# Layer norm, attention and a gated MLP: another order of the QKV calls, and the norm statistics of two blocks on ScalarE

## The chip, the cores and the metric

The kernel runs on one core of one Trainium2 chip. The metric is device microseconds (us) of one execution. Engine names in the profile: PE is TensorE, PEld its weight loads, DVE is VectorE, ACT is ScalarE, POOL is GpSimd, SP is SyncE (here it only issues DMAs).

## The reference

A layer of 2048 tokens with 576 channels: layer norm, attention of 32 heads in which each token looks at 8 keys (itself and every second token before it), a projection, a residual, then layer norm and a gated MLP of 4608 hidden units with a second residual. All in 32-bit floats.

```python
def _A_ref(x, wqkv, wo):
    H = 32; Dh = D // H            # 18 channels a head
    W, dil = 8, 2
    q, k, v = (x @ wqkv) ...       # split by head
    off = jnp.arange(W) * dil
    idx = pos[:, None] - off[None, :]
    ...
    attn = softmax(where(mask, einsum("bhsd,bhswd->bhsw", q, kg) * scale, -1e9))
    o = jnp.einsum("bhsw,bhswd->bhsd", attn, vg)
    return o... @ wo

def _B_ref(x, w_gate, w_up, w_down):
    return (sigmoid(x @ w_gate) * (x @ w_up)) @ w_down

h = x + _A_ref(_layernorm(x), A_wqkv, A_wo)
h2 = h + _B_ref(_layernorm(h), B_w_gate, B_w_up, B_w_down)
```

## The kernel before, in words

The tokens are split into even and odd ones (a key lies two tokens back, so the two sets never meet) and each set in halves: four blocks of 512 tokens, numbered 0 to 3, blocks 2 and 3 being the odd tokens. A block is four tiles of 128 tokens. Heads go in four groups of eight.

Matrix products are made of 32-bit operands split into a high and a low part (`split`: ACT copies the rounded high part, DVE subtracts it from the source), with three matmuls for each product (`tok_major`).

The stretch before the MLP works like this:

- `ln1(b, xb)` norms block b tile by tile. `ln_j` takes mean and variance on DVE (`bn_stats`, `bn_aggr`) and the power -1/2 on POOL. For blocks 0 and 1 DVE applies them. For blocks 2 and 3 (`on_act`) ACT applies them in two passes, one that subtracts the mean and one that multiplies, and a third short one copies the last 64 columns. Then PE transposes the tile (`tr_main`, `tr_rest`) and ACT and DVE split the result into `th` and `tl`.
- `qkv(b, g, T, w)` is one call: queries, keys and values of head group g for block b, four passes of 14 matmuls with 432 columns. ACT copies each pass to `ev`, and three DMAs of ACT's queue store the call in DRAM. (1, 0) is block 1, head group 0.
- `att_all` is attention as a generator. It takes items in a fixed order: (0,0), (0,1), (1,0), (0,2), (0,3), (1,1), (1,2), (1,3), each after its call. An item fetches its queries, keys (`kw`) and values (`vw`) from DRAM through SP's queue and runs nearly wholly on DVE, with operations of up to 2.6 us. Items of block 1 are spilled to DRAM by a DMA of POOL's queue (`o<-kw`). Between the passes of each call, `step(ag, n)` emits some steps of attention.
- `norm_under(b, xb, call, n)` emits the norm of block b between the passes of a call of another block. `heads` emits calls without a norm beside them.
- The weights of head group 2 can be split only once the last call that uses those of group 0 is emitted, since two groups fit; the same for group 3 after group 1.
- After the second pass of (2,3), `front` projects block 0 (`proj_j`), norms it and stores it (`x<-tok`). Then the MLP starts. Its first weights are loaded early (`wf`), the next (`wg`) by a DMA of POOL's queue. Attention items (1,1) to (1,3) that are not finished run on under the MLP, and block 1 is projected there.

The scheduler orders instructions on each engine by the order of emission, by priority (`tc.high_priority(n)` moves an instruction ahead by n places) and by its own estimate of when operands are ready. On the chip each engine and each DMA queue then runs in that fixed order.

Of the kernel before, what the change touches and what calls it, by code (L numbers as in the profile page):

```python
# [15 lines left out]
F32 = mybir.dt.float32  # L16
F32R = mybir.dt.float32r
AF = mybir.ActivationFunctionType
ALU = mybir.AluOpType
AX = mybir.AxisListType  # L20

P = 128
S = 2048
D = 576
# [6 lines left out]
NS = 4  # L31
TB = P * NS
DM = 512
DR = D - DM
DX = D + DR
# [5 lines left out]
EPS = 1e-5  # L41
# [11 lines left out]
HI = 400  # L53
# [7 lines left out]
def kernel(ctx, tc, x, wqkv, wo, wmlp, out):  # L61
    nc = tc.nc
    dve, act, pool, pe, sp = nc.vector, nc.scalar, nc.gpsimd, nc.tensor, nc.sync
# [9 lines left out]
    sm = ctx.enter_context(tc.tile_pool(name="sm", bufs=2))  # L73
# [12 lines left out]
    mhalf = cst.tile([P, 1], F32, name="mhalf")  # L86
# [16 lines left out]
    def split(hi, lo, src):  # L103
        act.activation(hi, src, AF.Copy)  # L104
        splits.append(dve.tensor_tensor(lo, src, f32(hi), ALU.subtract))  # L105

    def split_rest(t, src):
        act.activation(t, src, AF.Copy)
        dve.tensor_tensor(t[64:128], src[64:128], f32(t[64:128]), ALU.subtract)  # L109

    def pads(g):
        for e in range(2):
            for s in (kscr, vscr):
                a = s[e][g][0:LP, :]
                sp.dma_start(bass.AP(tensor=a.tensor, offset=a.offset,
                                     ap=[[LP * CG // 16, 16], [1, LP * CG // 16]]), zero)

    def ln_j(xj, xn, on_act):
        bs = sm.tile([P, 2, 6], F32, bufs=4, name="bs")
        mv = sm.tile([P, 2], F32, bufs=4, name="mv")  # L120
        rstd = sm.tile([P, 1], F32, bufs=4, name="rstd")
        for k in range(2):
            dve.bn_stats(bs[:, k], xj[:, k * DH2:(k + 1) * DH2])
        dve.bn_aggr(mv, bs)
        dve.tensor_scalar(rstd, mv[:, 1:2], EPS, None, ALU.add)
        pool.tensor_tensor(rstd, rstd, mhalf, ALU.pow)
        if on_act:
            nm = sm.tile([P, 1], F32, bufs=4, name="nm")
            dve.tensor_scalar(nm, mv[:, 0:1], -1.0, None, ALU.mult)
            act.activation(xn[:, :D], xj, AF.Identity, bias=nm)  # L130
            act.activation(xn[:, :D], xn[:, :D], AF.Copy, scale=rstd)
            act.activation(xn[:, D:DX], xn[:, DM:D], AF.Copy)
        else:
            dve.tensor_scalar(xn[:, :D], xj, mv[:, 0:1], rstd, ALU.subtract, ALU.mult)
            dve.tensor_copy(xn[:, D:DX], xn[:, DM:D])

    def tr_main(ps, xn):
        for c in range(4):
            pe.transpose(ps[:, c * P:(c + 1) * P], xn[:, c * P:(c + 1) * P], ident)
        return ps.rearrange("p (c n) -> p c n", c=4)  # L140

    def tr_rest(ps, xn):
        pe.transpose(ps[:, :P], xn[:, DM:DX], ident)
        return ps[:, :P]

    def tok_major(ps, n, th, tl, js, wh, wl):
        k = 0
        for c in range(4):
            for a, m in ((th, wh), (tl, wh), (th, wl)):
                pe.matmul(ps[:, :n], a[:, c, js], m[:, c], start=k == 0, stop=False)  # L150
                k += 1
        pe.matmul(ps[:, :n], th[:, 4, js], wh[:, 4], start=False, stop=False)  # L152
        return pe.matmul(ps[:, :n], th[:, 4, js], wl[:, 4], start=False, stop=True)  # L153
# [71 lines left out]
    def step(gen, n):  # L225
        for _ in range(n):
            if next(gen, END) is END:
                return

    def drain(gen):  # L230
        for _ in gen:
            pass
# [7 lines left out]
    def proj_j(bank, t, wos, th, tl, xn_tile, put, order=(0, 1)):  # L240
        oj = t[0]
        pv = tr_main(bank(), oj)
        with tc.high_priority(HI):
            split(th[:, 0:4], tl, pv)
        yield
        pv = tr_rest(bank(), oj)
        with tc.high_priority(HI):
            split_rest(th[:, 4], pv)
        yield
        for i in order:  # L250
            ps = bank()
            tok_major(ps, DH2, th, tl, slice(0, P), *wos[i])
            hs = t[1][:, i * DH2:(i + 1) * DH2]
            with tc.high_priority(HI):
                dve.tensor_tensor(hs, hs, ps[:, :DH2], ALU.add)
            yield
        xn = xn_tile()
        with tc.high_priority(HI):
            ln_j(t[1], xn, False)
        yield  # L260
        pv = tr_main(bank(), xn)
        with tc.high_priority(HI):
            put(pv, slice(0, 4))
        yield
        pv = tr_rest(bank(), xn)
        with tc.high_priority(HI):
            put(pv.unsqueeze(1), slice(4, 5))
        yield
# [18 lines left out]
    def th_tile():  # L287
        return xt.tile([P, 5, TB], F32R, tag="th", bufs=3, name="th")

    def tl_tile():  # L290
        return xt.tile([P, 4, TB], F32R, tag="tl", bufs=4, name="tl")
# [24 lines left out]
    def mm_tile():  # L316
        return psp.tile([P, 512], F32, tag="mm", bufs=3, name="mm")

    def acc_tile():
        return psp.tile([P, 512], F32, tag="acc", bufs=5, name="acc")  # L320

    def tok_tile(shape=(P, NS, DX)):
        return stk.tile(list(shape), F32, tag="tok", bufs=2, name="tok")

    def th3_tile(dt):
        return sar.tile([P, 5, TB], dt, tag="th3", name="th3")

    def ev_tile(shape):
        return sar.tile(shape, F32, tag="ev", bufs=2, name="ev")

    def load_x(b):
        e, hf = BLOCKS[b]
        t = sah.tile([P, NS, D], F32, bufs=2, name="h")
        for j in range(NS):
            sp.dma_start(t[:, j], xv[e, hf][:, j])
        return t

    def ln1(b, xb):
        th = th3_tile(F32R) if b == 3 else th_tile()
        tl = tl_tile()  # L340
        yield th, tl
        xn = tok_tile()
        for j in range(NS):
            js = slice(j * P, (j + 1) * P)
            pri = 2 * HI if b == 0 else HI if b > 1 else 0
            with tc.high_priority(pri):
                ln_j(xb[:, j], xn[:, j], b > 1)
            pv = tr_main(mm_tile(), xn[:, j])
            pr = tr_rest(acc_tile(), xn[:, j])
            with tc.high_priority(pri):  # L350
                split(th[:, 0:4, js], tl[:, :, js], pv)
                split_rest(th[:, 4, js], pr)
            yield

    def raw_w(g):
        if g == 3:
            wr = sah.tile([P, NS, D], F32, bufs=2, name="h").rearrange("p j d -> p (j d)")
            wr = wr[:, :QC].rearrange("p (c n) -> p c n", c=5)
        else:
            wr = swo.tile([P, 5, NQ], F32, tag="wo", name="wr")  # L360
        for c in range(5):
            sp.dma_start(wr[:, c], wqkv[g][:, c * NQ:(c + 1) * NQ])
        return wr
# [13 lines left out]
    def qkv(b, g, T, w):  # L377
        e, hf = BLOCKS[b]
        ev = ev_tile([P, 3, NS, CG])
        for j in range(NS):  # L380
            ps = acc_tile()
            passes.append(tok_major(ps, NQ, *T, slice(j * P, (j + 1) * P), w[:, 0], w[:, 1]))
            with tc.high_priority(HI):
                act.activation(ev[:, :, j], ps[:, :NQ].rearrange("p (t c) -> p t c", t=3), AF.Copy)  # L384
            yield
        r0 = LP + hf * TB
        with tc.high_priority(HI):
            act.dma_start(qscr[b][g], ev[:, 0].rearrange("p j c -> p (j c)"))
            for t, s in ((1, kscr), (2, vscr)):
                act.dma_start(s[e][g][r0:r0 + TB, :].rearrange("(p j) c -> p (j c)", p=P),  # L390
                              ev[:, t].rearrange("p j c -> p (j c)"))
        emitted.add((b, g))
# [29 lines left out]
    T = []  # L422

    def norm_under(b, xb, call, n):
        gl = ln1(b, xb)
        T.append(next(gl))
        for _ in call:
            step(ag, n)
            next(gl, END)
            step(ag, n)  # L430
        drain(gl)

    def heads(order, ws, n):
        for b, g in order:
            for _ in qkv(b, g, T[b], ws[g]):
                step(ag, n)

    xb = load_x(0)
    w = [qkv_w(0, raw_w(0))]
# [4 lines left out]
    xb = load_x(1)  # L444
# [3 lines left out]
    xb = load_x(2)  # L448
    norm_under(2, xb, qkv(1, 0, T[1], w[0]), 1)
    xb = load_x(3)  # L450
    wr = raw_w(2)
    norm_under(3, xb, qkv(2, 0, T[2], w[0]), 1)
    heads(((3, 0),), w, 2)
    w.append(qkv_w(2, wr))
    wr = raw_w(3)
    pads(2)
    heads(((1, 1), (0, 2), (2, 1), (3, 1)), w, 2)
    w.append(qkv_w(3, wr))
    pads(3)
    h = load_x(0)  # L460
# [649 lines left out]
    for c, (kind, p, f) in enumerate(items):  # L1110
        w, d = wc
# [116 lines left out]
```

## Time and profile before

| | |
|---|---|
| median of three runs | 1589.88 us (1587.89 to 1590.72) |
| profiled execution, first to last instruction (span) | 1589.2 us |
| granted TensorE clock, mean over the span | 0.993 |
| TensorE busy | 1553.3 us |
| VectorE busy | 1268.1 us |
| ScalarE busy | 869.2 us |
| GpSimd busy | 184.2 us |

The profile gives no time for the profiled execution beside its span; the median of the runs lies 0.7 us above that span. The busy time of an engine is a sum over the whole span. A wait names the engine and line that came last. A row of a timeline begins with its start and length in us, and ends with the idle time before it and what ended that, in brackets. "L104" is line 104 of the kernel; lines 104 and 105 are the two halves of `split`, so one line stands for many tiles and the tile's name tells them apart.

### The profile page before, as it was taken

How to read it: one execution, taken by the hardware profiler on the slowest of the kernel's cores; microseconds unless marked ns; L12 is line 12 of the kernel's file. 1: busy time of each engine (PE TensorE's matmuls, PEld its weight loads, DVE VectorE, ACT ScalarE, POOL GpSimd, SP SyncE). 2: the span in 40 equal slices, each digit the busy share in tenths (PEclk: the TensorE clock that was granted, in tenths of full speed). 3: DMA queues.
4: the chain of work that ended last, by engine and by line, in shares of the span. 5: the costliest groups of instructions: out<-in, count | busy, mean ns of one | idle time of the engine just before them, and what ended most of it. 6: DMA issues, size and time to landing. Idle time of an engine off the chain costs nothing.

```text
span 1589.2 us, 22383 instructions
## 1 busy us (share of the span) xinstructions
PE 1553.3 (98%) x8532; PEld 1381.6 (87%) x8532; DVE 1268.1 (80%) x1931; ACT 869.2 (55%) x1546; POOL 184.2 (12%) x230
## 2 busy tenths in 40 slices
PE   7999979999999999999989999999999999999998
PEld 6999968888888888888879988888888888888887
DVE  7999988959999999999546687876677776677755
ACT  4432234425555666656443255776677776677761
POOL 1000000011010001000101100122112112212210
PEclk9999999999999999999999999999999999999999
DMA  7664544346367565665764234899989999989983
GB/s 267 208 206 163 193 184 165 133 177 246 104 164 205 157 170 139 166 191 149 210 203 143 100 110 110 182 186 181 176 169 183 184 173 180 177 170 182 184 170 124
DMA packets 76892, 273.50 MB, mean 172 GB/s; under 512 B 8336, under 2 KB 14224, under 8 KB 75888
## 3 DMA queue, kind: packets, MB, share of 16 engines
q0 software_dynamic: 27792, 105.89, 36.3%
q1 hardware_dynamic: 41360, 146.06, 27.4%
q10 hardware_dynamic: 7632, 20.12, 3.3%
q8 instruction: 67, 1.10, 0.3%
q14 instruction: 41, 0.34, 0.1%
HBM read 145.88 MB, written 128.52 MB: 173 GB/s over the span
## 4 chain that ended last, share of the span: by engine, by line
PE 55%; issue 27%; POOL 7%; DVE 6%; DMA 4%; ACT 1%; SPq 0%; POOLq 0%; ACTq 0%; DVEq 0%
PE b L609 23%; PE dp L723 15%; POOL h L794 7%; PE acc L150 6%; PE b L616 4%; PE b L150 1%; PE bgp L150 1%; DMA wg<-in_wmlp_dram 1%; DVE pr L182 1%; DMA x<-tok 1%; DVE pr L208 1%; DVE lg L186 1%; PE acc L152 1%; DMA tail<-h 1%; PE acc L153 1%
## 5 line engine op out<-in xcount | busy, mean ns | idle before, releaser
L609 PE MATMUL b<-tl,w 128*128 128x512 f32 x1716 | 438.1, 395 | 9.1 <-ACT w L104 6.5
L609 PEld LDWEIGHTS b<-tl,w 128*128 128x128 f32 x1716 | 311.7, 189 | 66.5 <-ACT w L104 7.7
L609 PE MATMUL b<-th,w 128*128 128x512 f32 x1368 | 352.8, 393 | 0.4 <-DVE s L698 0.3
L609 PEld LDWEIGHTS b<-th,w 128*128 128x128 f32 x1368 | 249.8, 188 | 46.7 <-DVE s L698 0.7
L104 ACT ACTIVATE w<-wg 128x640 fp32r<-128x640 f32 (+2 forms) x197 | 117.0, 598 | 125.2 <-PE b L616 59.8
L791 ACT ACTIVATE ev<-dp 128x576 f32<-128x576 f32 x224 | 145.0, 647 | 61.8 <-PE dp L785 58.2
L616 PE MATMUL b<-th,w 128*128 128x512 f32 x572 | 177.0, 391 | 0.0
L794 POOL DMA_DIRECT2D h<-ev x128 | 110.2, 862 | 456.8 <-ACT ev L791 440.5
L105 DVE TENSOR_TENSOR w<-wg,w 128x640 fp32r<-128x640 f32 (+2 forms) x197 | 126.8, 649 | 38.7 <-ACT w L104 38.3
L150 PE MATMUL acc<-qw,th 128*128 128x432 f32 x512 | 155.7, 365 | 1.2 <-DVE th L109 0.9
L105 DVE TENSOR_TENSOR w<-tw,w 128x512 fp32r<-128x512 f32 x116 | 79.6, 687 | 81.1 <-ACT w L104 80.2
L616 PEld LDWEIGHTS b<-th,w 128*128 128x128 f32 x572 | 107.7, 188 | 23.1
L723 PE MATMUL dp<-d,h0h 128*128 128x288 f32 x640 | 119.0, 296 | 1.7 <-DVE tail L733 1.7
L723 PE MATMUL dp<-d,h1h 128*128 128x288 f32 x640 | 120.0, 297 | 0.0
L723 PEld LDWEIGHTS dp<-d,h0h 128*128 128x128 f32 x640 | 99.4, 189 | 5.5 <-DVE tail L733 2.0
L150 PEld LDWEIGHTS acc<-qw,th 128*128 128x128 f32 x512 | 97.2, 190 | 6.5 <-DVE th L109 1.1
L723 PEld LDWEIGHTS dp<-d,h1h 128*128 128x128 f32 x640 | 99.5, 190 | 2.9
L731 ACT ACTIVATE stage<-dp 128x576 f32<-128x576 f32 x96 | 61.7, 646 | 62.4 <-PE dp L723 62.3
L104 ACT ACTIVATE w<-tw 128x512 fp32r<-128x512 f32 x116 | 72.8, 628 | 41.3 <-PE b L609 40.9
L150 PE MATMUL acc<-qw,tl 128*128 128x432 f32 x256 | 92.8, 362 | 0.0
L384 ACT ACTIVATE ev<-acc 128x432 f32<-128x432 f32 x64 | 33.9, 531 | 104.4 <-PE acc L153 97.7
L182 DVE TENSOR_TENSOR pr<-kw,q 128x2304 f32<-128x2304 f32 x32 | 81.7, 2552 | 2.8 <-DMA kw<-k 2.6
(278 smaller groups left out, 2899.8 us busy)
## 6 DMA issues: line engine op xcount, KB each, us to landing
h<-ev POOLq DMA_DIRECT2D x96, 576.0 KB, 7.2
wg<-in_wmlp_dram SPq DMA_DIRECT2D x49, 928.0 KB, 5.2
h<-stage POOLq DMA_DIRECT2D x24, 1152.0 KB, 10.6
wg<-in_wmlp_dram SPq DMA_DIRECT2D x36, 640.0 KB, 4.1
kw<-k SPq DMA_DIRECT2D x16, 792.0 KB, 4.4
vw<-v SPq DMA_DIRECT2D x16, 792.0 KB, 5.5
wd<-in_wmlp_dram SPq DMA_DIRECT2D x18, 576.0 KB, 7.2
h<-ev POOLq DMA_DIRECT2D x32, 288.0 KB, 6.8
```

Of the source, the lines that this page charges most:

```text
L104: act.activation(hi, src, AF.Copy)
L105: splits.append(dve.tensor_tensor(lo, src, f32(hi), ALU.subtract))
L150: pe.matmul(ps[:, :n], a[:, c, js], m[:, c], start=k == 0, stop=False)
L152: pe.matmul(ps[:, :n], th[:, 4, js], wh[:, 4], start=False, stop=False)
L182: dve.tensor_tensor(pr, both(kw, u), q[:, us].unsqueeze(2).broadcast_to([P, 2, W, CG]), ALU.mult)
L384: act.activation(ev[:, :, j], ps[:, :NQ].rearrange("p (t c) -> p t c", t=3), AF.Copy)
L609: pe.matmul(ps, wt[:, a, k0 + c], xx[:, m + c], start=first and k == 0, stop=k == 5, skip_group_check=True)
L616: pe.matmul(ps, wt[:, a, k0], xx[:, 4], start=False, stop=a == 1, skip_group_check=True)
L723: pe.matmul(ps[:, i, :DH2], a[:, js], d[:, m, i * DH2:(i + 1) * DH2], start=k == 0, stop=k == n)
L731: act.activation(hv, ps, AF.Copy)
L791: act.activation(hs[:, k % 2], ps[:, :, :DH2], AF.Copy)
L794: pool.dma_start(hsev[:, u, k0:k + 1], hs[:, :k + 1 - k0], accum_op=ALU.add, max_dma_last_dim=8 * D)
```

## The change

Two things change.

The order of calls: (1,1) is called directly after (1,0), and the norm of block 3 is emitted under it instead of under (2,0). Then follow (2,0) and (3,0), the weights of group 2, and (2,1), (0,2), (3,1). The call (0,2) thereby moves from seventh to eighth place. The other calls keep their place, and attention its order of items.

The norm of blocks 2 and 3: DVE has no part in the statistics any more. ACT makes two passes over the tile that also sum along the row: a copy scaled by -1/576, whose sum is the negative mean, and a square with that mean added, whose sum is 576 times the variance. Their written output is discarded. POOL takes the power and multiplies the mean by it. A third pass of ACT applies both at once. The statistics of a tile are emitted one tile ahead of its scaling. The splits of blocks 2 and 3, and their norm, lose the priority that they had (`HI`).

```diff
-    def ln_j(xj, xn, on_act):
+    def ln_j(xj, xn):
...
-        if on_act:
-            nm = sm.tile([P, 1], F32, bufs=4, name="nm")
-            dve.tensor_scalar(nm, mv[:, 0:1], -1.0, None, ALU.mult)
-            act.activation(xn[:, :D], xj, AF.Identity, bias=nm)
-            act.activation(xn[:, :D], xn[:, :D], AF.Copy, scale=rstd)
-            act.activation(xn[:, D:DX], xn[:, DM:D], AF.Copy)
-        else:
-            dve.tensor_scalar(xn[:, :D], xj, mv[:, 0:1], rstd, ALU.subtract, ALU.mult)
-            dve.tensor_copy(xn[:, D:DX], xn[:, DM:D])
+        dve.tensor_scalar(xn[:, :D], xj, mv[:, 0:1], rstd, ALU.subtract, ALU.mult)
+        dve.tensor_copy(xn[:, D:DX], xn[:, DM:D])
+
+    def ln_stats(xj, junk):
+        mv = sm.tile([P, 2], F32, bufs=4, name="mv")
+        rstd = sm.tile([P, 1], F32, bufs=4, name="rstd")
+        act.activation(junk[:, :D], xj, AF.Copy, scale=-1.0 / D, accum_out=mv[:, 0:1])
+        act.activation(junk[:, :D], xj, AF.Square, bias=mv[:, 0:1], accum_out=mv[:, 1:2])
+        pool.tensor_scalar(rstd, mv[:, 1:2], 1.0 / D, EPS, ALU.mult, ALU.add)
+        pool.tensor_tensor(rstd, rstd, mhalf, ALU.pow)
+        pool.tensor_tensor(mv[:, 0:1], mv[:, 0:1], rstd, ALU.mult)
+        return mv[:, 0:1], rstd
+
+    def ln_scale(xj, nr, xn):
+        act.activation(xn[:, :D], xj, AF.Identity, bias=nr[0], scale=nr[1])
+        act.activation(xn[:, D:DX], xn[:, DM:D], AF.Copy)
...
+        pri = 2 * HI if b == 0 else 0
+        nr = []
         for j in range(NS):
             js = slice(j * P, (j + 1) * P)
-            pri = 2 * HI if b == 0 else HI if b > 1 else 0
+            while b > 1 and len(nr) < min(j + 2, NS):
+                nr.append(ln_stats(xb[:, len(nr)], xn[:, len(nr)]))
             with tc.high_priority(pri):
-                ln_j(xb[:, j], xn[:, j], b > 1)
+                if b > 1:
+                    ln_scale(xb[:, j], nr[j], xn[:, j])
+                else:
+                    ln_j(xb[:, j], xn[:, j])
...
     xb = load_x(3)
+    norm_under(3, xb, qkv(1, 1, T[1], w[1]), 1)
     wr = raw_w(2)
-    norm_under(3, xb, qkv(2, 0, T[2], w[0]), 1)
-    heads(((3, 0),), w, 2)
+    heads(((2, 0), (3, 0)), w, 2)
     w.append(qkv_w(2, wr))
     wr = raw_w(3)
     pads(2)
-    heads(((1, 1), (0, 2), (2, 1), (3, 1)), w, 2)
+    heads(((2, 1), (0, 2), (3, 1)), w, 2)
     w.append(qkv_w(3, wr))
```

More of the change, by code (lines that the diff above doesn't have):

```diff
@@ L258, in proj_j @@
         with tc.high_priority(HI):
-            ln_j(t[1], xn, False)
+            ln_j(t[1], xn)
         yield
```

## The prediction, made before the changed kernel was run

> **What bounds the kernel now.** I read the page first, then the waits of TensorE over the whole span, then windows of the stretch before the MLP, and last the chain and the timelines around the largest wait. From the page:
>
> ```profile
> span 1589.2 us, 22383 instructions
> ...
> PE 1553.3 (98%) x8532; PEld 1381.6 (87%) x8532; DVE 1268.1 (80%) x1931; ACT 869.2 (55%) x1546; POOL 184.2 (12%) x230
> ...
> kw<-k SPq DMA_DIRECT2D x16, 792.0 KB, 4.4
> ```
>
> TensorE (PE) is busy 1553.3 of 1589.2 us. The change neither adds nor removes a matmul, so it can act only on the other 35.9 us and on the granted clock. The waits of PE say where that idle time lies:
>
> ```profile
> PE mm L139 <- DVE tok L134: 9.5, 2, 9.1
> PE b L609 <- ACT w L104: 6.5, 1, 6.5
> ...
> PE b L609 <- DVE s L629: 2.5, 1, 2.5
> PE b L139 <- DMA oj<-o: 2.4, 1, 2.4
> ...
> PE mm L150 <- DVE tl L105: 1.3, 1, 1.3
> PE acc L150 <- DVE th L109: 0.9, 1, 0.9
> ```
>
> The first row is mostly the 9.1 us in which block 0 is loaded and normed; the change does not touch it. In reach are 6.5, 2.5, 2.4, 1.3 and 0.9 us. Windows place them and show the clock (columns: PE, PEld, DVE, ACT and POOL busy, PEclk, DMA share, GB/s):
>
> ```profile
> 20.00:60.00 40.00, 38.88 (x218) 36.37 (x217) 34.95 (x91) 25.23 (x58) 6.47 (x12) 1.00 0.81 278
> ...
> 77.00:181.50 104.50, 104.50 (x535) 99.86 (x534) 99.94 (x87) 29.67 (x63) 0.91 (x1) 1.00 0.54 185
> ...
> 228.00:232.00 4.00, 1.51 (x7) 0.93 (x5) 0.74 (x1) 0.00 (x0) 0.00 (x0) 1.00 0.99 411
> 232.00:236.00 4.00, 0.00 (x0) 0.00 (x0) 2.92 (x2) 3.32 (x5) 0.00 (x0) 0.54 0.89 355
> 236.00:246.00 10.00, 7.46 (x17) 5.57 (x18) 8.66 (x12) 3.10 (x6) 0.00 (x0) 0.50 0.17 44
> ...
> 320.00:326.00 6.00, 6.00 (x33) 5.43 (x32) 2.74 (x4) 1.95 (x4) 0.00 (x0) 0.72 1.01 399
> ```
>
> From 77 to 181.5 us PE is never idle, and VectorE (DVE) is 96% busy beside it. The hole is the hand-over to the MLP: PE stops at 229.5, waits 6.5 us, then 2.5 us more, and the clock is at half until 246. Its 7.46 us of work between 236 and 246 would have taken half that, so the hole costs 6.5 + 2.5 + 3.7 = 12.7 us. The 2.4 us wait before block 1's output projection is followed by 6 us at clock 0.72, or 1.7 us more: 4.1 in all. The chain and timelines show what ends the hole:
>
> ```profile
> 221.19 11.15 DMA x<-tok
> 232.36 0.69 ACT d L104
> ```
>
> ```profile
> 233.06 1.28 ACT L653 ACT_TABLE_LOAD   x1
> ...
> 235.24 2.08 ACT L104 ACTIVATE w<-wg 128x640 fp32r<-128x640 f32 x4 [0.29 <-DMA wg<-in_wmlp_dram]
> ```
>
> ```profile
> 224.00 0.76 POOL L221 DMA_DIRECT2D o<-kw  x1 [12.57 <-DVE kw L219]
> 224.78 0.57 POOL L565 DMA_DIRECT2D wg<-in_wmlp_dram  x1
> ```
>
> ```profile
> DMA packets 1198, 5.43 MB, mean 272 GB/s; under 512 B 144, under 2 KB 144, under 8 KB 1069
> ...
> x<-tok ACTq DMA_DIRECT2D x1, 1280.0 KB, 11.1
> ...
> vw<-v SPq DMA_DIRECT2D x1, 792.0 KB, 5.9
> ...
> o<-kw POOLq DMA_DIRECT2D x1, 288.0 KB, 8.5
> ```
>
> Two transfers gate it, almost together. The store of block 0's normed rows (x<-tok) frees memory that `d` needs, and ScalarE (ACT) stands in order behind that until 232.36. The next MLP weights land at 235.24; POOL issued them only at 224.78, behind the spill of attention (1,1), which waited for DVE. Both run in a burst of 5.43 MB (217 to 237) that fills the DMA engines at 0.41 MB/us (the 228 to 232 row).
>
> **The norm on VectorE and ScalarE.** DVE rows from 20 to 60, ACT rows from 25 to 80 us:
>
> ```profile
> L123 DVE BATCH_NORM_STATS2 bs<-h 128x6 f32<-128x288 f32 x23 | 9.3, 437 | 0.1
> ...
> L124 DVE BATCH_NORM_AGGREGATE mv<-bs 128x2 f32<-128x12 f32 x12 | 2.0, 189 | 0.0
> L125 DVE TENSOR_SCALAR rstd<-mv 128x1 f32<-128x1 f32 x12 | 1.5, 144 | 0.0
> ...
> L129 DVE TENSOR_SCALAR nm<-mv 128x1 f32<-128x1 f32 x8 | 1.0, 144 | 0.0
> ```
>
> ```profile
> L131 ACT ACTIVATE tok<-tok,rstd 128x576 f32<-128x576 f32 x8 | 6.0, 773 | 0.9 <-POOL rstd L126 0.9
> L130 ACT ACTIVATE tok<-h,nm 128x576 f32<-128x576 f32 x8 | 5.9, 772 | 0.0
> ```
>
> ```profile
> L126 POOL TENSOR_TENSOR rstd<-rstd,mhalf 128x1 f32<-128x1 f32 x11 | 5.9, 563 | 16.4 <-DVE nm L129 9.8 <-DVE rstd L125 5.2 <-DVE mv L124 1.4
> ```
>
> Removed from DVE for each tile of 128 tokens, by busy over count: 2 x 0.404 + 0.167 + 0.125 + 0.125 = 1.22 us, so 4.9 us a block and 9.8 us for both. ACT goes from two passes over 576 columns to three: 0.77 us more a tile, 6.2 us in all. No row of before has a pass that also sums. Taken as free it leaves 6.2; at a further 0.25 us for each of 16 sums (an estimate, a third of L130's 0.772, since only one number a partition is written) it is 10.2; less than 6.2 is excluded, as a sum takes nothing away. I take 8. POOL gets three small operations for one: 1.1 us more a tile at 0.56 each, beside an otherwise idle engine. Statistics run one tile ahead of the scaling, so this latency lies under the neighbour tile's passes; without that cover it would add about 1.1 us to a tile's way to PE.
>
> ACT has room for it: busy 25.2 of 40 us from 20 to 60, it would have some 33. What hides its lateness is the new order. Block 2 is normed under (1,0) and first used by (2,0), which now comes one call later. A call is 56 matmuls, at 104.50/535 = 0.195 us each: 10.9 us of PE work that needs neither block. The same holds for block 3 and (3,0). The splits of blocks 2 and 3 also lose their priority on DVE; the same 10.9 us cover that.
>
> **What VectorE gains.** Attention is a queue on DVE, one item after the other:
>
> ```profile
> 35.95 2.56 DVE L182 TENSOR_TENSOR pr<-kw,q 128x2304 f32<-128x2304 f32 x1 [2.58 <-DMA kw<-k]
> ...
> 130.72 2.55 DVE L182 TENSOR_TENSOR pr<-kw,q 128x2304 f32<-128x2304 f32 x1
> ...
> 180.86 0.76 DVE L219 TENSOR_TENSOR tok<-kw 128x576 f32<-128x576 f32 x1
> ...
> 222.92 0.76 DVE L219 TENSOR_TENSOR kw<-kw 128x576 f32<-128x576 f32 x1
> ```
>
> The first item starts when its keys arrive, at 35.95, after 2.58 us of idleness. Block 2's statistics run before that, so their 4.9 us become idle time, except that a tile or so of block 1's splits can move into the gap (1 us). Block 3's 4.9 us lie after it and count in full. The lead is 4.9 + 1 = 6 us; bounds 4.9 and 9.8. One thing caps it: (0,2) becomes the eighth call instead of the seventh.
>
> ```profile
> 108.82 0.33 SPq L170 DMA_DIRECT2D kw<-k  x1
> ```
>
> Its keys were fetched at 108.82. One call later is 119.8, landing after 4.4 us at 124.2, where before DVE began that item at 130.72. So the cap is 6.5 us, and 6 just fits. PE's 0.9 us wait for a split, which stood behind block 3's statistics, goes: -0.9, with 0 as the other end.
>
> Block 0's projection does not start sooner:
>
> ```profile
> 184.04 0.71 PE L139 MATMUL mm<-ident,tok 128*128 128x128 f32 x5
> ```
>
> Its input was written by 181.6, and PE came to it, in order and without a wait, at 184.04. So x<-tok stays near 221 less the 0.9; its neighbours move. Attention (1,1) ends at 217.7 instead of 223.7, and with it the spill, the weights queued behind it on POOL, and the fetch of the next values (vw). That takes 0.81 + 0.29 MB out of the burst, 1.1/0.41 = 2.7 us, and starts the weights 6 us sooner. x<-tok then lands about 3 us sooner (between 0, if the weights take the freed share, and 5). The wait shrinks from 6.5 to 3.5: -3. The half-clock stretch follows the gap; I take half of its 3.7, -1.9. The 2.5 us wait stays, as long attention operations still stand before the sum there.
>
> The Trainium skill, "TensorE: Matmul & The Clock Gate", Part 1, has the clock halve after an idle window of about 3.4 us. By it a gap just under that would cost no half clock at either place, and the sum would be 1.8 and 0.9 lower, near 1579.4. The trace speaks against leaning on it: 2.4 us of idleness were followed by 0.72.
>
> The projection of block 1 waits for the last attention item. DVE arrives there about 6 to 8 us sooner (it also loses part of its own wait for `d`), PE some 6 us sooner. I take half of the 4.1: -2.
>
> Sum: -0.9 - 3 - 1.9 - 2 = -7.8 from 1589.2 gives 1581.4. The median of the three runs, 1589.88, lies 0.7 above this span, so the forecast is 1582.1 us. With all bounds the good end is 0.9 + 1.3 + 12.7 + 4.1 = 19 us, or 1571; the poor end of the same mechanism is -0.9 alone, 1589. A tell from no change needs about 0.2%, or 3.2 us.
>
> **Rivals.** First, no gain that shows: x<-tok is tied to PE's order, not to DVE, and a mere reshuffle of the burst leaves it at 232. Then the lead stops at the hand-over and 0 to 3 us remain: 1587 to 1590, centre 1588.5. For it speaks that ACT waits for x<-tok, not for the weights (0.29 us); against it, the 1.1 MB that leave. Chance 0.20.
>
> Second, slower: the ScalarE chain of a tile (sum, squares, three steps on POOL, scaling) becomes the bound between 40 and 80 us. It decides once block 2's last split comes later than the new call's 10.9 us of cover, that is after about 67 us, or block 3's after about 78. ACT falling behind by its added 6 to 10 us, plus evictions waiting behind passes, would make PE wait some 6 us and then run two or three clock steps like the one after the 2.4 us wait (1.7 each): 6 + 4 = 10, less 1 to 3 us won later, about 1597.5. For it: ACT's passes bunch, and a planner that costs summing passes too low would put transposes in PE's queue too early. Against it: the cover, and 7 us of room in 20 to 60. Chance 0.22. The Trainium skill, "ScalarE: Activation LUTs", Rules for kernel authors, says to use VectorE rather than ScalarE for multiplies and adds, and so speaks against the change. The rows half agree: 1.22 us a tile leave DVE and 0.8 to 1.3 come to ACT, so nothing is won on the operation, only on whose time it is. A variant is that Square needs another table: 1.28 us a load (the row above) between Square and Exp.
>
> Third, a better hand-over: the hole closes nearly whole and the later wait too, 14 to 19 us, about 1573. It needs x<-tok 5 us sooner; only luck in DMA order gives that. Chance 0.06.
>
> **How the numbers follow.** The forecast has 0.52; faster by over 0.2% holds it, less a share in which under 3.2 us remain (0.03), plus the third rival: 0.55. Same, within 0.2%: 0.20 and that 0.03, so 0.23. Slower: 0.22. The range runs from 1573 to 1597: about one in ten is left out at each end. The forecast's own range is 1575 to 1586.
>
> **What would show it.** Right: DVE's first operation of (0,2) near 124.5, the end of (1,1) near 218, POOL's weights issued near 218.5, x<-tok landing before 230, and PE's wait for `w` near 3.5. Wrong: PE waits on transposes or on `th` between 40 and 80 us; a wait of DVE for the keys of (0,2); x<-tok still landing past 232; or another static order on PE, which would put block 0's projection elsewhere than at 184.

## The result, and the profile after

| kernel | median, us | runs |
|---|---|---|
| before | 1589.44 (1587.3 to 1593.26) | 8 |
| changed | 1593.81 (1591.15 to 1596.27) | 8 |

The ratio is 1.0025, with a 95% interval of 1.0017 to 1.0034. The change makes the kernel slower by some 4 us; the forecast was 1582.1 us. The profiled execution of the changed kernel has a span of 1591.9 us, and a second one of the same kernel 1593.0. For the kernel before the two spans are 1589.2 and 1586.4, so the execution that the prediction was reckoned from was the slower of these two.

The main waits of TensorE in the changed kernel (us in total, times, longest; "..." stands for rows left out). Line numbers have moved: L141 and L142 are ACT's last pass and short copy of the norm, L146 and L150 the transposes, L622 the MLP's matmuls.

```profile
...
PE b L622 <- ACT w L104: 2.9, 1, 2.9
PE mm L146 <- ACT tok L141: 2.9, 1, 2.9
PE mm L157 <- DVE tl L105: 2.2, 1, 2.2
PE acc L150 <- ACT tok L142: 2.0, 1, 2.0
PE b L146 <- DMA oj<-o: 2.0, 1, 2.0
PE b L622 <- DVE s L642: 1.8, 1, 1.8
...
PE acc L157 <- DVE qw L105: 1.2, 1, 1.2
```

The first of these rows was 6.5 us before: the hand-over to the MLP did improve. The second and fourth are new. They are TensorE waiting for the norm that now runs on ScalarE, 4.9 us together, and the 1.2 us for `qw` is new as well. The third, a split of block 0's projection, was 1.3 us. Windows of TensorE (stretch, its length, PE busy, granted clock, DMA share, GB/s) show where time went and came from, first the kernel before:

```profile
40.00:60.00 20.00, 18.88 (x109) 1.00 0.75 253
60.00:80.00 20.00, 20.00 (x111) 1.00 0.45 162
...
220.00:240.00 20.00, 10.86 (x45) 0.81 0.70 260
240.00:260.00 20.00, 20.00 (x86) 0.85 0.46 155
```

and the changed kernel:

```profile
40.00:60.00 20.00, 17.82 (x102) 1.00 0.65 213
60.00:80.00 20.00, 17.08 (x93) 1.00 0.57 182
...
220.00:240.00 20.00, 17.50 (x84) 1.00 0.72 261
240.00:260.00 20.00, 16.07 (x64) 0.83 0.38 138
```

Between 40 and 80 us TensorE loses 5.1 us where it lost 1.1. Read from its timeline, the fourth QKV call ends 5.0 us later than before, the tenth 6.0 and the sixteenth 9.7. Of the 3.7 us between the last two, 0.9 is the longer wait for the split of block 0's projection, 1.7 a stretch of half clock behind it (granted clock 0.72 from 194 to 200 us, 1.00 before) and 0.9 two waits for ScalarE's copies to `ev` (1.2 us, 0.3 before). In the second trace of the changed kernel the clock stays at 1.00 there. At the hand-over 6.4 us are idle (2.5 + 3.9) in place of 9.1, and less work follows at half clock: the first MLP product behind that wait is 6.1 us late and the four hundredth only 1.8. From there to the 3200th another 2.7 us go (4.5 us late). Of these, 1.5 go ahead of the 2000th, and the clock accounts for them: a wait of 4.0 us (3.8 before) is followed by twice as long a stretch of half clock, here first before, then changed:

```profile
820.00:830.00 10.00, 8.04 (x38) 0.83 0.56 213
```

```profile
820.00:830.00 10.00, 6.05 (x25) 0.66 0.60 244
```

The 1.2 us between the 2000th and the 3200th go without a wait and at full clock. The last 180 us give 1.9 back, among it a wait of 1.7 us that is gone, and the end is 2.7 us late. Two questions follow: what made the norm late, and what costs time in the MLP.

ScalarE's timeline around the two new waits (start, length, instruction; in brackets the idle time before it and what ended that):

```profile
55.83 0.42 ACT L203 ACTIVATE lg<-lg 128x256 f32<-128x256 f32 x1 [2.87 <-DVE lg L202]
56.16 0.85 ACT L141 ACTIVATE tok<-h,mv,rstd 128x576 f32<-128x576 f32 x1
...
59.45 0.26 ACT L142 ACTIVATE tok<-tok 128x64 f32<-128x64 f32 x1
...
68.70 0.87 ACT L141 ACTIVATE tok<-h,mv,rstd 128x576 f32<-128x576 f32 x1 [2.71 <-POOL mv L137]
```

In the first place ScalarE stands for 2.87 us in front of attention's exponential, whose input DVE has not finished, and the norm's passes are queued behind it. In the second it waits 2.71 us for GpSimd. GpSimd's rows say why:

```profile
39.84 2.94 POOL L136 TENSOR_TENSOR rstd<-rstd,mhalf 128x1 f32<-128x1 f32 x1
...
51.22 0.19 POOL L135 TENSOR_SCALAR rstd<-mv 128x1 f32<-128x1 f32 x1 [4.43 <-ACT tok L134]
51.50 0.55 POOL L136 TENSOR_TENSOR rstd<-rstd,mhalf 128x1 f32<-128x1 f32 x1
...
65.31 2.45 POOL L135 TENSOR_SCALAR rstd<-mv 128x1 f32<-128x1 f32 x1 [1.40 <-ACT tok L134]
```

```profile
39.81 2.56 DVE L189 TENSOR_TENSOR pr<-kw,q 128x2304 f32<-128x2304 f32 x1 [4.12 <-DMA kw<-k]
...
65.15 2.56 DVE L215 TENSOR_TENSOR pr<-vw,lg 128x2304 f32<-128x2304 f32 x1
```

A step of 0.19 us takes 2.45 and one of 0.55 takes 2.94, both times when a VectorE product with two inputs has begun just before; they end within 0.5 us of it. The Trainium skill, "GPSIMD Engine Reference", Specifications, says that GpSimd shares its SBUF interfaces with VectorE and contends with instructions of two SBUF inputs; the trace agrees. And attention itself starts at 39.81 in place of 35.95, waiting 4.12 us for its keys.

### The profile page after: what moved, and what is told of

It reads as the page before. It is cut to its first block, busy times and chain, and to the rows that moved or that the text cites. A ratio compares the mean times of both kernels' runs of the same rounds, so it can differ in the third digit from the quotient of the medians.

```text
span 1591.9 us, 22379 instructions
## 1 busy us (share of the span) xinstructions
PE 1555.0 (98%) x8532; PEld 1381.9 (87%) x8532; DVE 1262.8 (79%) x1891; ACT 872.1 (55%) x1568; POOL 193.2 (12%) x246
## 4 chain that ended last, share of the span: by engine, by line
PE 84%; DVE 8%; DMA 4%; ACT 2%; issue 1%; POOL 0%; SPq 0%; ACTq 0%; POOLq 0%; DVEq 0%
PE b L622 41%; PE dp L736 14%; PE dp L798 11%; PE b L629 8%; PE acc L157 6%; DMA wg<-in_wmlp_dram 2%; PE b L157 1%; PE bgp L157 1%; DVE lg L193 1%; DVE pr L189 1%; DVE pr L215 1%; DVE tl L105 1%; DVE w L105 1%; DMA o<-kw 0%; PE acc L159 0%
## 5 line engine op out<-in xcount | busy, mean ns | idle before, releaser
L622 PE MATMUL b<-tl,w 128*128 128x512 f32 x1716 | 437.0, 394 | 5.2 <-ACT w L104 2.9
L622 PEld LDWEIGHTS b<-tl,w 128*128 128x128 f32 x1716 | 311.1, 188 | 62.8 <-ACT w L104 3.4
L622 PE MATMUL b<-th,w 128*128 128x512 f32 x1368 | 353.3, 393 | 0.1
L622 PEld LDWEIGHTS b<-th,w 128*128 128x128 f32 x1368 | 249.8, 188 | 46.1 <-DVE s L642 0.5
```

What stands on the lines that cost most here:

```text
L622: pe.matmul(ps, wt[:, a, k0 + c], xx[:, m + c], start=first and k == 0, stop=k == 5, skip_group_check=True)
```

## The experiments

Each was timed in five rounds beside the kernel before on the same chip, unless it is called a trace alone.

**Order and norm apart.** e1 is the kernel before with only the new order of calls; e2 is the changed kernel with the old order.

```diff
e1, on the kernel before (e2 is the reverse, on the changed kernel):
     xb = load_x(3)
+    norm_under(3, xb, qkv(1, 1, T[1], w[1]), 1)
     wr = raw_w(2)
-    norm_under(3, xb, qkv(2, 0, T[2], w[0]), 1)
-    heads(((3, 0),), w, 2)
+    heads(((2, 0), (3, 0)), w, 2)
...
-    heads(((1, 1), (0, 2), (2, 1), (3, 1)), w, 2)
+    heads(((2, 1), (0, 2), (3, 1)), w, 2)
```

> The kernel before with the new order of calls alone: the norm of blocks 2 and 3 as before, on VectorE and with its priority. Theory A (the three-pass norm chain through ScalarE and GpSimd makes TensorE wait 5 us at 57 to 70 us): those waits for tok are absent here, TensorE reaches block 0's projection at 183 to 185 us as before, and the time is within 2 us of before. Theory B (the order of calls itself costs, because calls of group 2 and 3 and the weight splits fall elsewhere): TensorE reaches the projection some 4 to 6 us late here too, and the time is 3 to 5 us above before.

> The changed norm (three ScalarE passes, no priority) in the old order of calls. Theory A: the cover of one call (10.9 us) is gone, so TensorE waits more than the 5 us of the changed kernel before block 2's and block 3's first calls, 8 to 12 us in all, and the time is 6 to 12 us above before. Theory B: the waits of the changed kernel go with its order, and the time is at or below before.

e1: 1590.24 us, ratio 1.0007 (0.9999 to 1.0016). It has no wait for ScalarE's part of the norm, and its wait at the hand-over is the old one (6.4 us). The order by itself costs nothing that shows, and wins nothing. e2: 1591.8 us, ratio 1.0019 (1.0009 to 1.0028), with waits of 2.9 us for L141 and 2.3 for L142, and 6.2 at the hand-over. Neither of its expectations came: without the cover of a call the waits for the norm are no larger than with it (5.2 us against 4.9), and they still lie at the norm's transposes, none of them where block 2's or block 3's calls begin. The waits come with the norm on ScalarE, in either order. How much of e2's time they are is not shown by this pair, since e2 differs from the kernel before in the place of its tiles too (below). In these traces the shorter wait at the hand-over appears only with both parts.

**Priority, and the load of block 3.** e3 gives the norm and splits of blocks 2 and 3 their priority again. e4 answers for the late first attention: in the changed kernel SyncE issues block 3's load (29.82) ahead of the first keys (33.21), where before the keys went first (31.19).

```diff
e3:
-        pri = 2 * HI if b == 0 else 0
+        pri = 2 * HI if b == 0 else HI if b > 1 else 0
e4 (first_v[0] is the fetch of the first item's values):
-    xb = load_x(3)
+    with tc.issue_after(getattr(first_v[0], "ins", first_v[0])):
+        xb = load_x(3)
```

> The changed kernel with the old priority given back to the scaling and the splits of blocks 2 and 3. Theory C (ScalarE and VectorE serve other work first because the priority was dropped): TensorE's two waits for tok (2.0 and 2.9 us) go, the projection starts 4 to 5 us sooner, and the time is 3 to 5 us below the changed kernel. Theory A with its two causes, a GpSimd step stopped behind VectorE and ScalarE held by an exponential in its order: priority moves neither, the waits stay at 3 us or more, and the time is within 2 us of the changed kernel.

> The changed kernel with block 3's load pinned behind the first attention item's fetches of queries, keys and values. Theory D (that load goes ahead of them on SyncE's queue, so attention starts at 39.8 us instead of 35.9, and the exponential that ScalarE waits 2.9 us for comes late): attention starts by 37 us, ScalarE's wait for the exponential falls below 1 us, TensorE's 2.0 us wait behind it goes, and the time is 2 to 4 us below the changed kernel. If the late start does not matter: attention starts sooner, TensorE's waits stay as they are, and the time is within 1 us of the changed kernel.

e3: 1592.99 us, 1.0021 (1.0009 to 1.0034). Waits between 40 and 80 us:

```profile
PE acc L150 <- ACT tok L142: 1.2, 2, 0.7
PE mm L146 <- ACT tok L141: 1.2, 2, 0.9
```

Half of the wait is gone and the time hardly falls. e4: 1593.03 us, 1.0031 (1.0019 to 1.0042). Attention starts at 35.68, ScalarE no longer waits in front of the exponential (53.92), the wait for L142 falls from 2.0 to 1.0 us and that for L141 is still 2.6, and nothing is won. At this point waits alone did not explain the time.

**The GpSimd steps.** In e6 nothing of the norm of blocks 2 and 3 runs on GpSimd. It leaves out the division by the standard deviation of these blocks: the last pass takes the sum of squares itself as its scale.

```diff
-        rstd = sm.tile([P, 1], F32, bufs=4, name="rstd")
...
-        pool.tensor_scalar(rstd, mv[:, 1:2], 1.0 / D, EPS, ALU.mult, ALU.add)
-        pool.tensor_tensor(rstd, rstd, mhalf, ALU.pow)
-        pool.tensor_tensor(mv[:, 0:1], mv[:, 0:1], rstd, ALU.mult)
-        return mv[:, 0:1], rstd
+        return mv[:, 0:1], mv[:, 1:2]
```

> The changed kernel without its three small GpSimd steps: the last pass takes the variance itself as its scale, so the division by the standard deviation of blocks 2 and 3 is left out and the norm chain runs through ScalarE alone. Theory A1 (the GpSimd steps, stopped behind VectorE's two-input operations, make the chain late): the wait of 2.9 us of a transpose for L141's result before 69.6 us falls under 0.5, of the 2.0 us for L142's short copy some stays, the fourth QKV call ends 2 to 3 us sooner than in the changed kernel, and the time falls by 2 to 3 us, to about 1591. Theory A2 (ScalarE's own three passes and the exponential between them are late by themselves): the waits stay within 1 us of 5, the time stays at 1593 to 1594.

1592.34 us, ratio 1.0008 (0.9999 to 1.0017), where the changed kernel has 1.0025. Its only wait between 40 and 80 us is the one behind the exponential (L137 and L138 are here the last pass and the short copy), and the two last passes that the changed kernel ran at 65.11 and 68.70 now follow each other:

```profile
PE acc L146 <- ACT tok L138: 2.0, 1, 2.0
```

```profile
65.02 1.62 ACT L137 ACTIVATE tok<-h,mv 128x576 f32<-128x576 f32 x2
```

So the 2.9 us wait was the GpSimd steps, stopped behind VectorE's product. The fourth call ends 2.9 us sooner than in the changed kernel. The time falls by 1.5 us, a little less than expected, and the two intervals touch.

**All repairs, and the pace of the MLP.** e7 keeps one GpSimd step a tile (the power), with the small sums and products on ScalarE, and adds e3 and e4. The unedited kernels were traced again beside it.

```diff
+    epst = cst.tile([P, 1], F32, name="epst")
+    pool.memset(epst, EPS)
...
-        act.activation(junk[:, :D], xj, AF.Copy, scale=-1.0 / D, accum_out=mv[:, 0:1])
-        act.activation(junk[:, :D], xj, AF.Square, bias=mv[:, 0:1], accum_out=mv[:, 1:2])
-        pool.tensor_scalar(rstd, mv[:, 1:2], 1.0 / D, EPS, ALU.mult, ALU.add)
+        act.activation(junk[:, :D], xj, AF.Copy, scale=-1.0 / D ** 1.5, accum_out=mv[:, 0:1])
+        act.activation(junk[:, :D], xj, AF.Square, bias=mv[:, 0:1], scale=D ** -0.5,
+                       accum_out=mv[:, 1:2])
+        act.activation(rstd, mv[:, 1:2], AF.Identity, bias=epst)
         pool.tensor_tensor(rstd, rstd, mhalf, ALU.pow)
-        pool.tensor_tensor(mv[:, 0:1], mv[:, 0:1], rstd, ALU.mult)
+        act.activation(mv[:, 0:1], mv[:, 0:1], AF.Copy, scale=D ** 0.5)
+        act.activation(mv[:, 0:1], mv[:, 0:1], AF.Copy, scale=rstd)
```

> All repairs together: one GpSimd step a tile (the power) in place of three, the small additions and products on ScalarE, the high priority of the norm restored, block 3's load pinned behind the first attention's fetches; what is computed is the same. If the waits of the norm stage are what made the changed kernel slower, TensorE has under 1 us of waits between 55 and 75 us, the shorter wait of the hand-over (2.9 us for w) stays, and the time is 1588 to 1590, no slower than before. If the cost lies elsewhere (the pace of the long products of the second half, or later waits), it stays at 1592 to 1594 although those waits are gone.

> The changed kernel once more, unedited, for its trace alone. If the start-to-start gap of the 128x512 products of the MLP (231.08 ns from 1000 to 1550 us in the changed kernel, 230.26 in the one before) belongs to the program, it is 231.08 again and 226.75 between 360 and 560 us; if it is set anew in each execution, it may come out at 230.26 or 227.77.

> The kernel before once more, unedited, for its trace alone. If the gap of the MLP's products belongs to the program, it is 230.26 ns again from 1000 to 1550 us and 226.75 from 360 to 560; if it is set anew in each execution, it may come out at 231.08 or 227.77.

e7: 1590.19 us, 1.0004 (0.9993 to 1.0016): no loss shows any more. But it was expected to have under 1 us of waits for the norm, and it has 3.4 us of them between 40 and 80 us. With its tiles put back (e10, below) the same kernel has 3.8, the larger part of them in one wait of 3.1 us that ends at 58.99. There ScalarE stands for 1.85 us in front of an eviction that TensorE has not finished, and the sums of the next tile and the last pass that TensorE waits for (L147 in e10) come behind it:

```profile
PE mm L152 <- ACT tok L147: 3.8, 2, 3.1
```

```profile
55.95 0.53 ACT L405 ACTIVATE ev<-acc 128x432 f32<-128x432 f32 x1 [1.85 <-PE acc L166]
...
58.08 0.85 ACT L147 ACTIVATE tok<-h,mv,rstd 128x576 f32<-128x576 f32 x1
```

What e7 and e10 no longer have are the later waits, for `qw` and, at 226 to 229 us, for ScalarE's copies to `ev`. So the time does not follow the norm's waits alone. Nor are waits all of it. The traces give the mean gap from start to start of the MLP's 128x512 products where one directly follows another. From 1000 to 1400 us there is no wait and full clock, the order of the products is the same in all kernels, and yet:

| kernel | gap, ns |
|---|---|
| before; traced again; e1 | 230.3; 230.3; 230.3 |
| changed; traced again; e2, e3, e4, e6 | 231.1; 231.1; 231.1 each |
| e7 | 230.1 |

The same program gives the same gap in both of its traces, so the pace belongs to the program. What differs between the groups is no instruction of that stretch but the place of the tiles: the change drops the small tile `nm`, four buffers of 32 bytes a partition, and every later tile of SBUF lies 128 bytes lower; e7's new constant moves them up again by 32.

**The place of the tiles.** Four kernels move the tiles and leave everything else as it is; e9 and e11 are the kernel before.

```diff
e8, on the changed kernel (e10: [P, 24] on e7; e11: [P, 8] on the kernel before):
     mhalf = cst.tile([P, 1], F32, name="mhalf")
+    shift = cst.tile([P, 32], F32, name="shift")
+    pool.memset(shift, 0.0)
e9, on the kernel before:
-            nm = sm.tile([P, 1], F32, bufs=4, name="nm")
+            nm = bs[:, 0, 0:1]
```

> The changed kernel with 128 bytes a partition of unused constants, so that every SBUF tile behind them lies where it lay in the kernel before (the change drops the small tile nm, four buffers of 32 bytes, and all later tiles moved down by 128 bytes). Theory P (the place of the tiles sets the pace of the long products): the gap of the MLP's 128x512 products from 1000 to 1400 us falls from 231.1 back to 230.3 ns, that is 1.25 us less from the 2000th to the 3200th of them, and the time falls by 2 to 3 us, to 1591 to 1592; the waits of the norm stage (2.9 and 2.0 us) stay. Rival (the pace follows the instructions of the norm or the clock's history): 231.1 ns as before, time 1593 to 1594.

> The kernel before, with the negated mean kept in a place of bs that is free by then, so that nm is not allocated and every later tile lies 128 bytes lower, as in the changed kernel; the instructions are the same. Theory P: the gap rises from 230.3 to 231.1 ns and the time by 2 to 2.5 us over the kernel before, ratio about 1.0014, with no wait of TensorE changed. Rival: 230.3 ns and no difference.

> The kernel with all repairs (one GpSimd step a tile, priority, block 3's load later) with 96 bytes of unused constants, so that its tiles lie where those of the kernel before lie. It led the kernel before by 1.2 us at the hundredth product of the MLP and by 0.6 at the four hundredth, and lost 2.4 us between there and the two thousandth. If that loss is the place of its tiles, the lead stays to the end: 1588 to 1589.5. If not, 1590 as without the bytes.

> The kernel before with all tiles 32 bytes higher (32 bytes of unused constants), nothing else. Theory P lets the pace take another value here, the sign not known: the gap from 1000 to 1400 us somewhere between 229.5 and 231.5 ns and the time within 3 us of before. Rival: 230.3 ns and no difference.

| kernel | place of the tiles | gap, ns | us | ratio, 95% interval |
|---|---|---|---|---|
| changed | 128 lower | 231.1 | 1593.81 | 1.0025 (1.0017 to 1.0034) |
| e8: changed, tiles back | as before | 230.3 | 1592.85 | 1.0013 (1.0004 to 1.0023) |
| e9: before, tiles 128 lower | 128 lower | 231.1 | 1592.42 | 1.0014 (1.0003 to 1.0024) |
| e11: before, tiles 32 higher | 32 higher | 229.6 | 1590.34 | 1.0001 (0.9992 to 1.0010) |
| e10: all repairs, tiles back | as before | 230.3 | 1588.98 | 0.9992 (0.9981 to 1.0003) |

The windows from 1000 to 1400 show it as a count of products (the number behind the x). Before, changed, e8, e9, one line each:

```profile
1000.00:1400.00 400.00, 400.00 (x2159) 1.00 0.91 180
```

```profile
1000.00:1400.00 400.00, 400.00 (x2153) 1.00 0.90 178
```

```profile
1000.00:1400.00 400.00, 400.00 (x2159) 1.00 0.91 179
```

```profile
1000.00:1400.00 400.00, 400.00 (x2152) 1.00 0.91 180
```

Both directions agree: 128 bytes lower loses six or seven products in 400 us, and putting the tiles back restores them. e9 has the waits of the kernel before (6.5 us at the hand-over, none for ScalarE's norm) and is 2 us slower all the same, from its tiles alone. In e8 the pace came back as expected and the time fell by 1 us where 2 to 3 were expected. e11 shows that the gap is not the whole pace: its gap is the shortest, 229.6 ns, but the step from a 512-column product to one of 288 columns takes 231.5 ns there and 229.0 before, the step back 133.8 and 132.0, and in all it makes the same 2159 products from 1000 to 1400 us. Its time is that of before. In e7 these steps cost more too, and it makes 2154 products, nearly as few as the changed kernel.

**What is left.** e12 keeps the changed kernel's priority and load, with the tiles back and one GpSimd step. e13 is e10 with the tiles 32 bytes higher, where e11 had the shortest gap.

```diff
e12, on e10:
-        pri = 2 * HI if b == 0 else HI if b > 1 else 0
+        pri = 2 * HI if b == 0 else 0
...
-    with tc.issue_after(getattr(first_v[0], "ins", first_v[0])):
-        xb = load_x(3)
+    xb = load_x(3)
e13, on e10:
-    shift = cst.tile([P, 24], F32, name="shift")
+    shift = cst.tile([P, 32], F32, name="shift")
```

> The changed kernel with its tiles where the kernel before has them and with one GpSimd step a tile (the power), the small sums and products on ScalarE; priority and block 3's load as in the changed kernel. If the GpSimd steps behind VectorE's two-input operations are the other half of the loss, the ratio falls from 1.0013 (tiles put back, three steps) to 1.0000 or below, time 1588.5 to 1590.5, and the fourth QKV call ends 2 to 3 us sooner than with three steps. If the priority and the load are what counted in the repaired kernel, it stays at 1592 to 1593 with 4 to 5 us of waits for the norm's results between 55 and 75 us.

> The kernel with all repairs, its tiles 32 bytes higher than those of the kernel before, where the products of the MLP ran at 229.6 ns from 1000 to 1400 us. If that pace comes with the place again, the gap is 229.6 and the time 0 to 2 us under the 1589.0 of the place of before, 1587 to 1589. Rival: the pace of 229.6 was paid for elsewhere (1590.3 there, no faster than before), and the time is 1589 to 1590.

e12 went the other way: 1595.22 us, 1.0036 (1.0024 to 1.0048), the slowest of all. Its waits (L147 and L148 are here the last pass and the short copy) and windows:

```profile
PE acc L156 <- ACT tok L148: 3.8, 2, 3.4
PE mm L152 <- ACT tok L147: 3.2, 1, 3.2
```

```profile
40.00:60.00 20.00, 16.61 (x87) 0.91 0.69 222
60.00:80.00 20.00, 16.34 (x78) 0.83 0.38 118
```

```profile
55.66 0.42 ACT L209 ACTIVATE lg<-lg 128x256 f32<-128x256 f32 x1 [3.42 <-DVE lg L208]
55.98 0.24 ACT L148 ACTIVATE tok<-tok 128x64 f32<-128x64 f32 x1
56.13 0.28 ACT L140 ACTIVATE rstd<-mv,epst 128x1 f32<-128x1 f32 x1
```

The small steps that left GpSimd now stand on ScalarE behind the same exponential, which waits 3.42 us because attention starts at 38.64. With priority and load repaired (e10) attention starts at 34.97 and that exponential runs at 52.61 without a wait. So the expectation that the GpSimd steps alone are the other half fell. The reading that fits these traces is that it counts how late the chain comes in ScalarE's queue, with GpSimd's stops as one way of making it late; at one place of the tiles e10 and e12 differ only in priority and load, and by some 6 us. e12 also shows the further price: with waits of over 3 us the clock falls to 0.91 and 0.83.

e13: 1588.21 us, 0.9985 (0.9975 to 0.9994). It beats the kernel before, and e11, at the same place of the tiles, does not; so what is won comes from the repaired change. It is not won at the norm, where e13 still waits 3.8 us, but behind it. Against the two traces of the kernel before, its fourth call ends 1.8 and 2.9 us late, its sixteenth 1.4 and 2.5, and its four hundredth MLP product starts 2.7 and 0.8 us ahead. Its windows at the hand-over (the kernel before: 10.86 at 0.81 and 20.00 at 0.85):

```profile
220.00:240.00 20.00, 14.72 (x60) 0.87 0.52 203
240.00:260.00 20.00, 20.00 (x101) 0.96 0.67 248
```

## Why the prediction was wrong

**The failed step** is the hiding of ScalarE's lateness; the sum has no term for it. The prediction put the norm's chain behind one call's cover of 10.9 us and GpSimd's steps "beside an otherwise idle engine" at 0.56 us each. Measured, these steps take 0.19 and 0.55 us alone and up to 2.45 and 2.94 beside a two-input product of VectorE, and the chain lies in ScalarE's order behind an exponential that waits for attention. TensorE paid 4.9 us of waits, and not where block 2's calls begin: the first calls after the norm have no wait, but the transposes of the norm itself stand in TensorE's order between the passes of the call above them, here (1,1). The cover left the transposes bare; e2, without it, has the same waits. This is the second rival, at the place that the prediction named for it (40 to 80 us) and with 4.9 us for the 6 it gave, though at the transposes, which it names too, and without its condition: block 3's last split ends at 76.3 us, not after 78. Its clock price of 4 us did not come at that place in the changed kernel, where the clock stays at 1.00 from 40 to 80 us, but in others (0.83 from 60 to 80 us in e8 and in e12). The load of another table that it named as a variant does not occur between 3 and 239 us.

**ScalarE's added time** was between 6.2 and 10.2 us, taken as 8. Its rows give 5.4 + 1.6 for the first sums, 6.2 + 1.6 for the second and 6.9 for the scaling, 21.7 us for the eight tiles where two passes took 11.9: 9.8 more. Each sum costs an instruction of its own:

```profile
L134 ACT ACTIVATE tok<-h,mv 128x576 f32<-128x576 f32 x8 | 6.2, 780 | 0.0
...
L134 ACT ACTIVATION_READ_ACCUMULATOR tok<-h,mv 128x1 f32 x8 | 1.6, 204 | 0.0
```

**VectorE's lead** was to be 6 us, so that (0,2) would begin near 124.5. It began at 128.68, 2.0 sooner than before. The first item started 3.9 us later: block 3's load passed its keys on SyncE's queue. The prediction weighed what the idle time before the first item could take in and not what the reordering did to the fetch that ends it. That is not the whole of it, for in e4 the first item starts at 35.68 again and (0,2) only at 127.80. With priority restored as well it begins 5 to 8 us sooner than before (125.6 in e7, 124.56 in e13, 122.91 in e10), each time after VectorE waited 1.4 to 3.0 us for its keys, so the lead was there to be had, up to the cap that the prediction named, and its conditions were missed.

**PE's 0.9 us wait** for the split went, as forecast, and larger ones took its place.

**The hand-over** came out nearly as argued. x<-tok takes 7.59 us in place of 11.15, and TensorE's wait is 2.9 us where 3.5 was forecast. The granted clock from 230 to 250 us is 0.83 in place of 0.66, and the work done at half clock falls from 7.46 to 5.04 us, so 1.2 us are saved there and not 1.9:

```profile
230.99 7.59 DMA x<-tok
```

It is issued at 230.99 in place of 221.19, because TensorE arrives 9.7 us late; a better hand-over was spent on a later arrival. Attention (1,1) ends at 219.3 (forecast 217.7) and GpSimd issues the weights at 222.43 (forecast 218.5).

**Block 1's projection** was to give 2 us. Its wait did not shrink (2.4 us before, 2.0 and 0.4 now). The half clock behind it is gone in the first trace of the changed kernel and there again in the second (0.96 from 300 to 340 us, as before), so this term is not shown to have come.

**The place of the tiles** was in no step of the prediction, and by the middle values it is about half of the loss: 1.0014 alone, and 1.0025 against 1.0013 in the changed kernel. The intervals are wide (1.0003 to 1.0024 alone) and those of the changed kernel and e8 overlap, so the share is rough; that the place counts is shown by the counts of products. The dropped line `nm = sm.tile(...)` stood in the diff as a saving on VectorE only.

What stays open: why 128 bytes change the pace. The traces show that they do, in both directions, and that the gaps vary from product to product between 223 and 237 ns in a pattern that comes back; no run tells what in the addresses counts. How much of the repaired kernel's gain is priority and how much the load was not separated with the tiles in place. How the rest of the loss divides between the norm's 4.9 us of waits and the later waits and half clocks is argued from the traces, not shown by an experiment, since the repaired kernels keep 3.4 to 3.8 us of the former and are not slower.

## What to carry to other kernels

Ask of every cover which instructions it covers: a call of slack in front of a norm's consumers does nothing for the transposes that stand inside it in TensorE's order. Small steps on an idle engine are not free where that engine can be stopped by its neighbour, as GpSimd was here, and the next step stands in an ordered queue; count the ways that a chain crosses between engines, not only its busy time. And when an edit drops or adds even a small tile, put its bytes back before comparing times at the level of 0.2%.

## What the runs showed of the hardware that was not expected

The place of SBUF tiles changes the pace of products that wait for nothing: the gap of 128x512 products that follow each other is 229.6, 230.3 and 231.1 ns from 1000 to 1400 us for tiles 32 bytes higher, at their place and 128 lower, the same within 0.1 ns in every trace of a place. The shortest gap is not the best pace: all products counted, the first two places come out alike (2158 to 2161 in 400 us), and 128 lower gives 2151 to 2154. The Trainium skill, "SBUF — State Buffer", SBUF: two separate sides, has contention among the engines at the port pair of VectorE and GpSimd alone and TensorE's ports never waiting. No run here shows whether another engine has a part in the difference.

A wait of under 3 us can halve the clock or not. The 2.9 us wait near 70 us left the clock at 1.00 from 60 to 80 in the changed kernel; in e8, with the same wait, it was

```profile
60.00:80.00 20.00, 17.05 (x79) 0.83 0.53 187
```

The Trainium skill, "TensorE: Matmul & The Clock Gate", Part 1, tells of a free-running window of 3.4 us, which fits that the same wait falls differently from one kernel to another; that an idle window of 3.4 us is needed does not fit the 2.9 us here.
